# An attention and mixture-of-experts kernel: the copy of transposed q puts tokens in natural order, and each store of the output becomes one block

## The chip, the core and the metric

The kernel runs on one core of a Trainium2 chip. The core has TensorE (PE) for matrix products, VectorE (DVE), ScalarE (ACT) and GpSimd (POOL) for the rest, SyncE (SP), which here only issues transfers, and 16 DMA engines that move data between HBM and the on-chip memory SBUF. TensorE writes its results to PSUM, eight banks of 2 KB in each of 128 partitions. The metric is the device time of one execution in microseconds (us).

## What is computed

```python
q_s = softmax(q, axis=-1)            # q, k, v: (8 batches, 8 heads, 576 tokens, 64)
k_s = softmax(k, axis=2)             # over the tokens
kv  = einsum('bhsd,bhse->bhde', k_s, v)
x   = einsum('bhsd,bhde->bhse', q_s, kv)      # then laid out as (8, 576, 512)

pooled = x.mean(axis=1)              # one row for each batch
logits = pooled @ w_gate             # 8 experts
e      = argmax(logits);  gate = softmax(logits)[e]
out[b] = gate * (relu(x[b] @ w1[e]) @ w2[e])  # w1: 512 x 1024, w2: 1024 x 512
```

The inputs and the output are float32. Each batch picks one expert, and only that expert's weights are loaded.

## The kernel before

**Layout of the tokens.** A load of q, k or v brings four heads of one batch (half a batch, `i`) into a tile of 128 partitions. `pair_src` puts token `9 p + j` of a head into partition `p` (64 of them for each of two heads), at place `j`. So a partition holds nine neighbouring tokens, and the loads read long contiguous rows. TensorE transposes q for each `j` (L150): 64 columns, one for each `p`, go to columns `64 j + p` of a PSUM bank. VectorE copies the 576 columns as they lie to the tile `qt` in SBUF (L157). From there on the columns of x, and so of h, stand in the order `(j, p)`, not in that of the tokens.

**A batch.** `attention(b)` is a generator of ten steps, with a `yield` after each; `moe(b)` has thirteen. Attention: exp of q and k on ScalarE (`eq`, `ek`, L118 and L123); the cast of v on GpSimd (`va`, L129); row sums, reciprocals and the scaling of `eq` on VectorE (`qs`, `qsi`, `eq`, L134 to L137). Then for each half `i`: the transposes (L150, bank `tk`) and the two copies `qt` (L157); k times v (L164), the scaled `kv` (L171, L173); x (L182, L183) and its copy `xt` to SBUF with the sum for the mean (L184, L188). Then the logits (L196), the expert's number (L205), the loads of its weights as float16, issued by GpSimd (`w1_sb`, `w2_sb`, L211 to L217), and the gate (L225 to L231). MoE: eight blocks of 128 hidden units (`hm`, L243, 512 tokens; `ht`, L248, the last 64), each followed by a relu on ScalarE or VectorE in turn (`hsb`, L253 and L255), and then five blocks of output rows (`po`, L264), which ScalarE scales by the gate into `osb` (L269) and SP stores (L271).

**The store.** The five blocks of a batch have 128 columns each, the last 64. A block of 128 columns holds two values of `j`, so its rows are two sets of 64 tokens, each with a step of nine tokens in the output:

```python
out_j = out.rearrange("b (p j) d -> b j p d", j=J)
...
js = slice(2 * st, min(2 * st + 2, J))
nc.sync.dma_start(out=out_j[b, js], in_=osb[0:rows])
```

**The order.** The first two batches' attention runs alone (the opening). Then iteration `b` runs the steps of `moe(b)` in turn with those of `attention(b + 2)`, until in iterations 6 and 7 `moe` is alone. This order is fixed for TensorE; the other engines' order is made by a scheduler. Buffers bound how far things run ahead: three input tiles of each kind (half a batch each), three `eq`, `ek` and `va`, so exp and softmax run up to three half-batches ahead of the transposes; three sets of weights; two banks `hm`, two `tk`, one `x`, two `po`; four `osb`. On SP the loads of batches 0 to 5 stand ahead of the first stores, then come the loads of batch 6, the stores of batch 1, the loads of batch 7, and only stores after that.

Of the kernel before, what the change touches and what calls it, by code (L numbers as in the profile page):

```python
# [10 lines left out]
FP16 = mybir.dt.float16  # L11
# [8 lines left out]
def kernel(  # L20
# [12 lines left out]
    nc = tc.nc  # L33

    B, H, S, Dh = q.shape
    D, E = moe_w_gate.shape
    F = moe_w1.shape[2]
    J = S // 64
# [18 lines left out]
    def bank(tag, bufs):  # L57
        return psum.tile([128, 512], FP32, name=tag, tag=tag, bufs=bufs)
# [33 lines left out]

        return t[b].rearrange("(i n g) (p j) d -> i (g p) n (j d)", i=2, n=2, p=64)[i]


    out_j = out.rearrange("b (p j) d -> b j p d", j=J)

    state = {}
    nv = [0]

# [9 lines left out]
    def attention(b, tiles, roomy):  # L110
# [5 lines left out]
        for i in range(2):  # L116
            eq = e_pool.tile([128, J, 2, Dh], FP16, name="eq")
            nc.scalar.activation(  # L118
                out=eq.rearrange("p j n d -> p n j d"),
                in_=tiles["q", i].rearrange("p n (j d) -> p n j d", j=J), func=AF.Exp,  # L120
# [3 lines left out]
                out=ek.rearrange("p j n d -> p n j d"),  # L124
                in_=tiles["k", i].rearrange("p n (j d) -> p n j d", j=J), func=AF.Exp,
# [4 lines left out]
                out=va[:, :, 1:].rearrange("p j (n d) -> p n j d", n=2),  # L130
                in_=tiles["v", i].rearrange("p n (j d) -> p n j d", j=J),
# [6 lines left out]
                out=eq, in0=eq, in1=qsi.unsqueeze(3).to_broadcast([128, J, 2, Dh]), op=ALU.mult,  # L138
# [5 lines left out]
        for i in range(2):  # L144
            eq, ek, va = eqs[i], eks[i], vas[i]
            tps = [bank(t_tag, 2) for g in range(2)]
            for j in range(J):
                for g in range(2):
                    r = slice(64 * g, 64 * g + 64)
                    nc.tensor.transpose(  # L150
                        out=tps[g].bitcast(FP16)[:, 64 * j:64 * j + 64],
                        in_=eq[r, j], identity=ident[r, r],
                    )
            qts = []
            for g in range(2):
                qt = qt_pool.tile([128, S], FP16, name="qt")
                nc.vector.tensor_copy(out=qt, in_=tps[g].bitcast(FP16)[:, 0:S])  # L157
                qts.append(qt)
            yield
            kps = [bank("tk", 2) for g in range(2)]  # L160
            for j in range(J):
                for g in range(2):
                    r = slice(64 * g, 64 * g + 64)
                    nc.tensor.matmul(  # L164
                        kps[g][:, 0:129], lhsT=ek[r, j], rhs=va[r, j],
                        start=(j == 0), stop=(j == J - 1),
                    )
            kvs = []
            for g in range(2):
                icv = kv_pool.tile([128, 1], FP32, name="icv")  # L170
                nc.vector.reciprocal(out=icv, in_=kps[g][:, 0:1])  # L171
                kv = kv_pool.tile([128, 128], FP16, name="kv")
                nc.vector.scalar_tensor_tensor(  # L173
                    out=kv, in0=kps[g][:, 1:129], scalar=icv, in1=blkmask, op0=ALU.mult, op1=ALU.mult,
                )
                kvs.append(kv)
            yield
            for g in range(2):
                c = 2 * i + g
                px = bank(x_tag, x_bufs)  # L180
                pxt = kps[g][:, 192:256]
                nc.tensor.matmul(px, lhsT=kvs[g], rhs=qts[g][:, 0:SM], start=True, stop=True)  # L182
                nc.tensor.matmul(pxt, lhsT=kvs[g], rhs=qts[g][:, SM:S], start=True, stop=True)  # L183
                nc.vector.tensor_tensor_reduce(  # L184
                    out=xt[:, c, 0:SM], in0=px, in1=ones_f32.to_broadcast([128, SM]),
                    scale=1.0, scalar=0.0, op0=ALU.mult, op1=ALU.add, accum_out=pooled[:, c:c + 1],
                )
                nc.vector.tensor_tensor_reduce(  # L188
                    out=xt[:, c, SM:S], in0=pxt, in1=ones_f32.to_broadcast([128, ST]),
                    scale=1.0, scalar=pooled[:, c:c + 1], op0=ALU.mult, op1=ALU.add,  # L190
                    accum_out=pooled[:, c:c + 1],
                )
                yield
# [15 lines left out]
        for i in range(2):  # L209
            for h in range(2):  # L210
                nc.gpsimd.dma_start(  # L211
                    out=w1_sb[64 * h:64 * h + 64, 2 * i:2 * i + 2, :], in_=w1_src[i, h]
# [22 lines left out]
    def moe(b):  # L235
        xt, gate, w1_sb, w2_sb = state.pop(b)
        hsb = h_pool.tile([128, NF, S], FP16, name="hsb")
        pht = bank("ht", 1)
        for fc in range(NF):
            phm = bank("hm", 2)  # L240
            fsl = slice(fc * 128, (fc + 1) * 128)
            for c in range(ND):
                nc.tensor.matmul(  # L243
                    phm, lhsT=w1_sb[:, c, fsl], rhs=xt[:, c, 0:SM],
                    start=(c == 0), stop=(c == ND - 1),
                )
            for c in range(ND):
                nc.tensor.matmul(  # L248
                    pht[:, fc * ST:(fc + 1) * ST], lhsT=w1_sb[:, c, fsl], rhs=xt[:, c, SM:S],
                    start=(fc == 0 and c == 0), stop=(fc == NF - 1 and c == ND - 1),  # L250
                )
            if fc % 2 == 0:
                nc.scalar.activation(out=hsb[:, fc, 0:SM], in_=phm, func=AF.Relu)  # L253
            else:
                nc.vector.tensor_single_scalar(out=hsb[:, fc, 0:SM], in_=phm, scalar=0.0, op=ALU.max)  # L255
            yield
        nc.scalar.activation(
            out=hsb[:, :, SM:S], in_=pht.rearrange("p (c s) -> p c s", c=NF), func=AF.Relu
        )
        for st in range(5):  # L260
            rows = 128 if st < 4 else ST
            po = bank("po", 2)
            for fc in range(NF):
                nc.tensor.matmul(  # L264
                    po[0:rows], lhsT=hsb[:, fc, st * 128:st * 128 + rows], rhs=w2_sb[:, fc, :],
                    start=(fc == 0), stop=(fc == NF - 1),
                )
            osb = o_pool.tile([128, D], FP32, name="osb")
            nc.scalar.mul(osb[0:rows], po[0:rows], gate[0:rows])  # L269
            js = slice(2 * st, min(2 * st + 2, J))  # L270
            nc.sync.dma_start(out=out_j[b, js], in_=osb[0:rows])  # L271
            yield

    def drain(gen):
# [7 lines left out]
    with tc.manual_schedule(engines={ET.PE}):  # L282
        for b in range(AHEAD):
            drain(attention(b, ins.pop(b), True))
        for b in range(B):
            n = b + AHEAD
            att = iter(())
            if n < B:
                if n not in ins:
                    ins[n] = loads(n)  # L290
                att = attention(n, ins.pop(n), False)
                next(att)
            for step, _ in enumerate(moe(b)):
                next(att, None)
            drain(att)
# [30 lines left out]
```

## Time and profile before

| | |
|---|---|
| time, median of 3 runs | 341.39 us (339.92 to 342.43) |
| the profiled execution, its own time | 341.65 us |
| its span in the profile | 340.0 us |
| mean granted clock of TensorE | 0.85 of full speed |
| moved by the DMA | 54.81 MB, 161 GB/s over the span |
| of it inputs and output (queue q1) | 37.75 MB |
| of it weights, as written (queue q0) | 16.78 MB |

A row of the profile's timeline reads: start in us, duration in us, engine, line, operation, output<-inputs, partitions x elements, count, and in brackets the idle time of the engine just before with what ended it. A row of the groups reads: line, engine, operation, shape, count | busy us, mean ns of one | idle us before. A row of the list of waits reads: engine and line that waited <- what it waited for: us in total, times, the longest. A row of the table of stretches reads: from:to, length, then busy us and count for PE, PEld (TensorE's weight loads), DVE, ACT and POOL, then granted clock, mean busy share of the 16 DMA engines, and GB/s. Overlapping packets can take that share over 1. In the chain, a step is what the last instruction was waiting for, followed back to the start.

### The profile page before, as it was taken

The numbers are of one execution on the slowest core, as the hardware profiler recorded it, in microseconds if no ns is written. First come the engines' busy times: TensorE is split into PE (matmuls) and PEld (weight loads), VectorE is DVE, ScalarE is ACT, GpSimd is POOL, SyncE is SP. The second block draws the span as 40 slices with busy tenths as digits, with TensorE's granted clock in tenths as the row PEclk, the third lists the DMA queues.
The fourth block names the chain that finished last, engine by engine and source line by source line (L and its number), as shares of the span: only waits on it lengthen the run. The fifth ranks groups of instructions, "written<-read, shape, count | busy, mean of one in ns | idle before, by whom it ended". The sixth has DMA issues, their size and how long they took to land.

```text
span 340.0 us, 4144 instructions
## 1 busy us (share of the span) xinstructions
PE 193.5 (57%) x1552; PEld 95.5 (28%) x1552; DVE 123.6 (36%) x365; ACT 89.6 (26%) x130; POOL 52.1 (15%) x73
## 2 busy tenths in 40 slices
PE   0344387880068930889107895960769885479400
PEld 0223144440024420344103443530335341134100
DVE  3699949510058110780106816710236020011000
ACT  2644235210044300442004434210123230123100
POOL 1325261330001410014100141040000400000000
PEclk9999999995559985699755999996779998599955
DMA  7999999999619791199811149179121781112111
GB/s 262 396 391 378 278 294 280 290 284 285 139 65 332 197 187 36 58 338 223 149 36 64 41 80 196 43 140 166 37 67 52 140 150 38 65 51 66 51 64 42
DMA packets 31508, 54.81 MB, mean 161 GB/s; under 512 B 2304, under 2 KB 10496, under 8 KB 31488
## 3 DMA queue, kind: packets, MB, share of 16 engines
q1 hardware_dynamic: 17856, 37.75, 31.4%
q0 software_dynamic: 13056, 16.78, 29.3%
q8 instruction: 12, 0.20, 0.2%
q10 hardware_dynamic: 576, 0.02, 0.1%
q14 instruction: 8, 0.07, 0.1%
HBM read 61.88 MB, written 9.44 MB: 210 GB/s over the span
## 4 chain that ended last, share of the span: by engine, by line
DMA 48%; DVE 19%; PE 18%; ACT 5%; issue 2%; SPq 1%; ACTq 1%; POOL 0%; DVEq 0%; POOLq 0%
DMA out_dram<-osb 45%; PE hm L243 8%; DVE qs L134 5%; PE po L264 5%; DVE eq L137 4%; DVE xt L184 3%; ACT osb L269 2%; DMA wg_sb<-in_moe_w_gate_dram 2%; DVE hsb L255 2%; ACT eq L118 2%; PE x L182 1%; DMA v_in<-in_v_dram 1%; DVE kv L173 1%; SPq L271 1%; ACT hsb L253 1%
## 5 line engine op out<-in xcount | busy, mean ns | idle before, releaser
L243 PE MATMUL hm<-xt,w_sb 128*128 128x512 f16 x256 | 74.5, 421 | 60.9 <-ACT hsb L253 60.9
L264 PE MATMUL po<-w_sb,hsb 128*128 128x512 f16 (+1 forms) x320 | 77.8, 393 | 22.9 <-ACT osb L269 22.9
L269 ACT ACTIVATE osb<-po,gate 128x512 f32<-128x512 f32 (+1 forms) x40 | 27.2, 686 | 151.6 <-DMA out_dram<-osb 120.8
L264 PEld LDWEIGHTS <-hsb 128*128 128x128 f16 (+1 forms) x320 | 31.0, 103 | 61.0 <-issue 31.3
L243 PEld LDWEIGHTS <-w_sb 128*128 128x128 f16 x256 | 22.5, 105 | 88.0 <-issue 72.6
L134 DVE TENSOR_REDUCE qs<-eq 128x18 f32<-128x1152 f16 x16 | 21.5, 1345 | 64.9 <-ACT eq L118 64.9
L129 POOL CAST va<-v_in 128x1152 f16<-128x1152 f32 x16 | 19.7, 1239 | 132.7 <-PE tk L164 82.2
L255 DVE TENSOR_SCALAR hsb<-hm 128x512 f16<-128x512 f32 x32 | 22.1, 690 | 44.6 <-PE hm L243 44.0
L211 POOL DMA_DIRECT2D w_sb<-in_moe_w_dram x32 | 19.3, 623 | 81.6 <-DVE gt L225 39.6
L253 ACT ACTIVATE hsb<-hm 128x512 f16<-128x512 f32 x32 | 18.8, 588 | 41.8 <-PE hm L243 41.8
L157 DVE COPY qt<-tk 128x576 f16<-128x576 f16 x24 | 9.9, 453 | 52.7 <-PE tk L150 52.7
L248 PEld LDWEIGHTS <-w_sb 128*128 128x128 f16 x256 | 17.7, 104 | 18.1 <-issue 5.4
L137 DVE TENSOR_TENSOR eq<-eq,qsi 128x1152 f16<-128x1152 f16 x16 | 21.8, 1360 | 0.1
L118 ACT ACTIVATE eq<-q_in 128x1152 f16<-128x1152 f32 x16 | 18.6, 1160 | 9.8 <-DMA q_in<-in_q_dram 5.7
L123 ACT ACTIVATE ek<-k_in 128x1152 f16<-128x1152 f32 x16 | 18.5, 1157 | 7.5 <-PE tk L164 4.2
L248 PE MATMUL ht<-xt,w_sb 128*128 128x64 f16 x256 | 19.2, 200 | 0.0
L184 DVE CUSTOM_DVE_ANT_0 xt<-x,ones_f 128x512 f16<-128x512 f32 x24 | 16.4, 684 | 6.6 <-PE tk L183 6.6
L182 PE MATMUL x<-qt,kv 128*128 128x512 f16 x24 | 10.8, 449 | 11.6 <-DVE kv L173 7.0
L164 PE MATMUL tk<-va,ek 64*128 64x129 f16 x288 | 13.8, 246 | 2.9 <-DVE pooled L188 1.9
L164 PEld LDWEIGHTS <-ek 64*128 64x128 f16 x288 | 10.5, 108 | 4.1 <-issue 2.1
L150 PEld LDWEIGHTS <-eq 64*128 64x128 f16 x288 | 6.4, 103 | 12.6 <-issue 11.8
L182 PE MATMUL po<-qt,kv 128*128 128x512 f16 x8 | 4.4, 612 | 9.3 <-DVE kv L173 9.3
(49 smaller groups left out, 106.1 us busy)
## 6 DMA issues: line engine op xcount, KB each, us to landing
q_in<-in_q_dram SPq DMA_DIRECT2D x16, 576.0 KB
k_in<-in_k_dram SPq DMA_DIRECT2D x16, 576.0 KB
v_in<-in_v_dram SPq DMA_DIRECT2D x16, 576.0 KB
w_sb<-in_moe_w_dram POOLq DMA_DIRECT2D x32, 256.0 KB, 10.6
w_sb<-in_moe_w_dram POOLq DMA_DIRECT2D x16, 512.0 KB, 20.7
out_dram<-osb SPq DMA_DIRECT2D x32, 256.0 KB
out_dram<-osb SPq DMA_DIRECT2D x8, 128.0 KB
wg_sb<-in_moe_w_gate_dram ACTq DMA_DIRECT2D x4, 4.0 KB
```

Source lines behind the costliest of these rows:

```text
L118: nc.scalar.activation(out=eq.rearrange("p j n d -> p n j d"), in_=tiles["q", i].rearrange("p n (j d) -> p n j d", j=J), func=AF.Exp,)
L129: nc.gpsimd.tensor_copy(out=va[:, :, 1:].rearrange("p j (n d) -> p n j d", n=2), in_=tiles["v", i].rearrange("p n (j d) -> p n j d", j=J),)
L134: nc.vector.tensor_reduce(out=qs, in_=eq, op=ALU.add, axis=AX.X)
L137: nc.vector.tensor_tensor(out=eq, in0=eq, in1=qsi.unsqueeze(3).to_broadcast([128, J, 2, Dh]), op=ALU.mult,)
L164: nc.tensor.matmul(kps[g][:, 0:129], lhsT=ek[r, j], rhs=va[r, j], start=(j == 0), stop=(j == J - 1),)
L184: nc.vector.tensor_tensor_reduce(out=xt[:, c, 0:SM], in0=px, in1=ones_f32.to_broadcast([128, SM]), scale=1.0, scalar=0.0, op0=ALU.mult, op ...
L243: nc.tensor.matmul(phm, lhsT=w1_sb[:, c, fsl], rhs=xt[:, c, 0:SM], start=(c == 0), stop=(c == ND - 1),)
L248: nc.tensor.matmul(pht[:, fc * ST:(fc + 1) * ST], lhsT=w1_sb[:, c, fsl], rhs=xt[:, c, SM:S], start=(fc == 0 and c == 0), stop=(fc == NF - ...
L253: nc.scalar.activation(out=hsb[:, fc, 0:SM], in_=phm, func=AF.Relu)
L255: nc.vector.tensor_single_scalar(out=hsb[:, fc, 0:SM], in_=phm, scalar=0.0, op=ALU.max)
L264: nc.tensor.matmul(po[0:rows], lhsT=hsb[:, fc, st * 128:st * 128 + rows], rhs=w2_sb[:, fc, :], start=(fc == 0), stop=(fc == NF - 1),)
L269: nc.scalar.mul(osb[0:rows], po[0:rows], gate[0:rows])
```

## The change

The copy out of PSUM now reads column `64 j + p` and writes column `9 p + j`, so `qt`, x and h have the tokens in natural order. The source is read in steps of 64 elements, the destination written in sequence. A block of output rows is then 128 (or 64) neighbouring tokens, and the store writes them as one contiguous block.

```diff
-    out_j = out.rearrange("b (p j) d -> b j p d", j=J)
...
-                nc.vector.tensor_copy(out=qt, in_=tps[g].bitcast(FP16)[:, 0:S])
+                nc.vector.tensor_copy(
+                    out=qt.rearrange("q (p j) -> q p j", j=J),
+                    in_=tps[g].bitcast(FP16)[:, 0:S].rearrange("q (j p) -> q p j", j=J),
+                )
...
-            js = slice(2 * st, min(2 * st + 2, J))
-            nc.sync.dma_start(out=out_j[b, js], in_=osb[0:rows])
+            nc.sync.dma_start(out=out[b, st * 128:st * 128 + rows, :], in_=osb[0:rows])
```

The number of instructions stays the same on each engine. The order of TensorE, ScalarE, GpSimd and SP stays too; lines of the changed kernel are numbered up to three lower. On SP, around the first stores (`out_dram<-osb`, with the shape of the destination), there stands before:

```order
L106 DMA k_in<-in_k_dram 128x2x576
L106 DMA v_in<-in_v_dram 128x2x576
L271 DMA out_dram<-osb 2x64x512 x4
L271 DMA out_dram<-osb 64x512
L106 DMA q_in<-in_q_dram 128x2x576
```

and now:

```order
L103 DMA k_in<-in_k_dram 128x2x576
L103 DMA v_in<-in_v_dram 128x2x576
L270 DMA out_dram<-osb 128x512 x4
L270 DMA out_dram<-osb 64x512
L103 DMA q_in<-in_q_dram 128x2x576
```

Nothing has moved; the four 128-row stores of each batch have another shape, and the 64-row store has the same one.

On VectorE the scheduler orders the opening differently. After the second half of batch 0 is transposed, there stands before:

```order
L157 COPY qt<-hm 128x576 x2
L134 TENSOR_REDUCE qs<-eq 128x18
L171 RECIPROCAL icv<-tk 128x1 x2
L136 RECIPROCAL qsi<-qs 128x18
L173 SCALAR_TENSOR_TENSOR kv<-tk,icv,blkmask 128x128 x2
L137 TENSOR_TENSOR eq<-eq,qsi 128x1152
L184 ISA xt,pooled<-po,ones_f_100 128x512
```

and now:

```order
L154 COPY qt<-hm 128x576 x2
L171 RECIPROCAL icv<-tk 128x1 x2
L131 TENSOR_REDUCE qs<-eq 128x18
L173 SCALAR_TENSOR_TENSOR kv<-tk,icv,blkmask 128x128 x2
L133 RECIPROCAL qsi<-qs 128x18
L184 ISA xt,pooled<-po,ones_f_100 128x512
```

The scaling of a later `eq` has moved behind the copies `xt` there. There are a few more such exchanges up to the gate of batch 1; as many `qs` and `eq` stand ahead of that gate as before (seven of each), and from there on the order is the same.

## The prediction

> **What bounds the kernel now.** I read the page first: busy shares, DMA queues, chain.
>
> ```profile
> PE 193.5 (57%) x1552; PEld 95.5 (28%) x1552; DVE 123.6 (36%) x365; ACT 89.6 (26%) x130; POOL 52.1 (15%) x73
> q1 hardware_dynamic: 17856, 37.75, 31.4%
> q0 software_dynamic: 13056, 16.78, 29.3%
> DMA out_dram<-osb 45%; PE hm L243 8%; DVE qs L134 5%; PE po L264 5%; DVE eq L137 4%; DVE xt L184 3%; ACT osb L269 2%; DMA wg_sb<-in_moe_w_gate_dram 2%; DVE hsb L255 2%; ACT eq L118 2%; PE x L182 1%; DMA v_in<-in_v_dram 1%; DVE kv L173 1%; SPq L271 1%; ACT hsb L253 1%
> ```
>
> No engine is busy for more than 57% of the span, and the 16 DMA engines together for 60.7% (31.4 + 29.3). Yet 45% of the chain that ended last is the output stores. The list of waits, by total, says who suffers:
>
> ```profile
> ACT osb L269 <- DMA out_dram<-osb: 120.8, 14, 23.8
> ...
> PE hm L243 <- ACT hsb L253: 60.9, 7, 20.7
> ```
>
> ScalarE waits 120.8 us for an osb buffer that a store still reads. Behind that osb in ScalarE's queue stands the next batch's first relu (hsb), and TensorE, out of its two hm banks, waits 60.9 us for it. Why stores are slow shows in the table of stretches (the columns after the five engines are granted clock, DMA share, GB/s):
>
> ```profile
> 20.00:30.00 10.00, 3.01 (x38) 1.85 (x40) 9.54 (x28) 4.23 (x6) 2.31 (x3) 1.00 1.05 390
> 110.00:120.00 10.00, 10.00 (x61) 4.46 (x61) 1.49 (x11) 3.14 (x6) 3.90 (x6) 1.00 0.84 208
> 290.00:300.00 10.00, 6.18 (x20) 2.29 (x20) 0.00 (x0) 1.95 (x3) 0.00 (x0) 0.69 0.13 51
> 324.00:330.00 6.00, 0.00 (x0) 0.00 (x0) 0.00 (x0) 0.00 (x0) 0.00 (x0) 0.50 0.13 51
> ```
>
> At 20 to 30 us only loads run: 1.05 of 16 engines, 390 GB/s, so 23 GB/s an engine. At 324 to 330 only stores run: 0.13 x 16 = 2.1 engines and 51 GB/s, 24.5 GB/s an engine. The engines are not slow; a store keeps two of them busy. A 128-row store (262,144 B) takes 262,144 / 51 GB/s = 5.14 us. Late in the kernel the period of five stores is the distance of two 64-row osb's, both held by a store:
>
> ```profile
> 302.10 0.68 ACT L269 ACTIVATE osb<-po,gate 64x512 f32<-64x512 f32 x1 [4.18 <-DMA out_dram<-osb]
> ...
> 323.26 0.68 ACT L269 ACTIVATE osb<-po,gate 64x512 f32<-64x512 f32 x1 [4.18 <-DMA out_dram<-osb]
> ```
>
> It is 21.16 us, of which four 128-row stores take 20.56. The fifth, of 64 rows, gets 0.6 us; on two engines it would need 2.57. It is the one store that already is one block of rows, so the row order decides, not the direction of the transfer.
>
> The page "DMA: Bandwidth & Descriptors" of the Trainium skill, section "Why a DMA increments its semaphore by 16 and not by 1", says that a transfer runs on the largest number of engines up to 16 that divides the slowest dimension of both access patterns: 2 for a destination of 2 x 64 x 512, 16 for 128 x 512. The 2.1 busy engines agree; that 128-row stores spread no run here shows yet.
>
> **The change, part by part.**
>
> **The stores.** The destination goes from 2 x 64 x 512 to 128 x 512; 32 of 40 stores change. At 390 GB/s one takes 0.7 us, and even shared with loads some 2 us, against a new osb every 1.80 us with four buffers. I take it that ScalarE's 120.8 us of waits go, and TensorE's with them. What is late next is the work itself, so I rebuild the span from stretches without store waits. Unhindered is iteration 0 (MoE of batch 0 beside attention of batch 2):
>
> ```profile
> 44.60 1.89 PE L243 MATMUL hm<-xt,w_sb 128*128 128x512 f16 x4
> ...
> 49.26 1.16 PE L164 MATMUL tk<-va,ek 64*128 64x129 f16 x18
> ...
> 56.09 1.04 PE L243 MATMUL hm<-xt,w_sb 128*128 128x512 f16 x4
> ...
> 66.25 5.47 PE L264 MATMUL po<-w_sb,hsb 128*128 128x512 f16 x24
> 71.66 1.04 PE L243 MATMUL hm<-xt,w_sb 128*128 128x512 f16 x4
> ...
> 74.20 0.70 PE L164 MATMUL tk<-va,ek 64*128 64x129 f16 x18
> ```
>
> It runs from 44.60 to 71.66: 27.06 us. Its start is slow: from the first hm to the first tk (L164) takes 49.26 - 44.60 = 4.66 against 74.20 - 71.66 = 2.54 an iteration later, and that tk group 1.16 against 0.70. Warm, the iteration is 27.06 - 2.12 - 0.46 = 24.5. Later iterations of the trace start slow too, since TensorE idles in the store waits (granted clock 0.50 at 324 to 330 us); in a stretch with TensorE busy throughout (110 to 120) it is 1.00, so I count them warm.
>
> Softmax of q runs three half-batches ahead, so the second half of iteration 4 and all of iteration 5 have none. In iteration 5 the second half is
>
> ```profile
> 254.87 1.04 PE L243 MATMUL hm<-xt,w_sb 128*128 128x512 f16 x4
> ...
> 268.69 1.04 PE L243 MATMUL hm<-xt,w_sb 128*128 128x512 f16 x4
> ```
>
> 13.82 us long, against 71.66 - 56.09 = 15.57 in iteration 0: 1.75 less for each such half. Iterations 6 and 7 are MoE alone:
>
> ```profile
> 306.25 1.03 PE L243 MATMUL hm<-xt,w_sb 128*128 128x512 f16 x4
> ...
> 308.21 1.03 PE L243 MATMUL hm<-xt,w_sb 128*128 128x512 f16 x4
> ```
>
> Two hm blocks take 1.96, so eight take 7.8; three po blocks take 71.66 - 66.25 = 5.41, so five take 9.0: 16.8 us.
>
> **The copy of q (L157).** It now reads PSUM in steps of 64 elements. No row shows such a read.
>
> ```profile
> L184 DVE CUSTOM_DVE_ANT_0 xt<-x,ones_f 128x512 f16<-128x512 f32 x24 | 16.4, 684 | 6.6 <-PE tk L183 6.6
> L157 DVE COPY qt<-tk 128x576 f16<-128x576 f16 x24 | 9.9, 453 | 52.7 <-PE tk L150 52.7
> L188 DVE CUSTOM_DVE_ANT_0 xt<-tk,ones_f,pooled 128x64 f16<-128x64 f32 x32 | 8.8, 281 | 2.2
> L137 DVE TENSOR_TENSOR eq<-eq,qsi 128x1152 f16<-128x1152 f16 x16 | 21.8, 1360 | 0.1
> ```
>
> Low end: 453 ns as now. High end: 1360, the longest VectorE row. Between them, PSUM reads that get no fast rate: 684 ns for 512 elements and 281 for 64 are 0.90 ns an element and 223 fixed, so 741 for 576. I take 741, the nearest rows: +0.29 us a copy, 32 copies.
>
> Here a rule of the Trainium skill speaks against the change: "VectorE: DVE Perf Modes", section "What auto-detection actually checks", grants the paired rate only where every 16-bit tensor has step 1, which this read loses. By its cycle table (section on the TRN2 errata) the copy goes from an estimated 425 ns (the row says 453) to 725; the sum would be under 1 us lower than with 741.
>
> In the first 44 us VectorE is busy 9.54 of 10, so eight copies cost 8 x 0.29 = 2.3 us there. The scheduler also reorders softmax steps there, but as many of them stand ahead of batch 1's gate; I count that as nothing, with 2 us either way. In an iteration, where a copy matters shows in the second half of iteration 0:
>
> ```profile
> 56.18 0.82 DVE L157 COPY qt<-tk 128x576 f16<-128x576 f16 x2 [0.50 <-PE tk L150]
> 57.16 0.69 DVE L255 TENSOR_SCALAR hsb<-hm 128x512 f16<-128x512 f32 x1 [0.16 <-PE hm L243]
> ...
> 59.33 0.51 DVE L173 SCALAR_TENSOR_TENSOR kv<-tk,icv,blkmask 128x128 f16<-128x128 f32 x2
> ```
> ```profile
> 59.64 0.39 PE L182 MATMUL x<-qt,kv 128*128 128x512 f16 x1 [0.68 <-DVE kv L173]
> ```
>
> Two copies grow by 0.58; 0.16 of it hides in the wait of hsb for TensorE; the remaining 0.42 moves hsb, qs and kv, and TensorE, already 0.68 us idle for kv, waits that much longer. So 0.42 for each half with softmax. In the three halves without, VectorE has a qs (1.35 us) less to do, which covers it: nothing.
>
> **The first stores.** SP issues in program order:
>
> ```profile
> 67.43 2.94 SPq L106 DMA_DIRECT2D v_in<-in_v_dram  x1
> 70.46 29.38 SPq L271 DMA_DIRECT2D out_dram<-osb  x5
> ```
> ```profile
> 63.94 0.69 ACT L269 ACTIVATE osb<-po,gate 128x512 f32<-128x512 f32 x1 [2.27 <-PE po L264]
> ```
> ```profile
> 75.00:80.00 5.00, 0.00 (x0) 0.00 (x0) 0.00 (x0) 0.00 (x0) 1.16 (x1) 0.78 1.09 273
> ```
>
> The first osb is ready at 64.6, but its store goes out at 70.5, behind the loads of batch 5, and the DMA is full (1.09) until 80. The new store waits behind those three loads: 3 x 590 KB at 273 GB/s is 6.5 us, so it lands near 78, and the fifth osb, wanted at about 75, is some 3 us late. TensorE covers part with two hm blocks (2.5 us). I take 2 us once, between 0 and 6.
>
> **The end.** After the last po: osb 0.69, then a store that has the engines to itself. No row shows one. At 2.1 engines' rate it would take 2.6 us, and a whole round of loads took
>
> ```profile
> 106.39 4.73 DMA v_in<-in_v_dram
> ```
>
> 4.73 from issue to landing. I take 3 us, together 3.7.
>
> **Sum.** 44.6 + 2.3 = 46.9 to the first MoE matmul; iteration 0: 27.06 + 0.84 = 27.9; 1 to 3: 3 x (24.5 + 0.84) = 76.0; 4: 24.5 - 1.75 + 0.42 = 23.2; 5: 24.5 - 3.5 = 21.0; 6 and 7: 33.6; first stores 2; end 3.7. That is 234.3 us of span. The profiled execution took 341.65 for a span of 340.0, so 1.65 on top: **236 us**. It stands 0.3 above the median of 341.39, so nothing is corrected.
>
> **Rivals.**
>
> *The strided read is dearer than one element a step.* At 1360 ns the copy adds 0.91: 5.0 more in the opening, (1.82 - 0.16 - 0.42) = 1.24 more in each of nine halves, about 0.5 in the three others: 236 + 5.0 + 11.2 + 1.5 = 254. For it: nothing here reads PSUM in steps. Against: the rows that read PSUM one element at a time, at 0.90 ns each.
>
> *The DMA becomes the bound.* 60.7% of 340 us is 206 us of all 16 engines; at the full share of 1.09 that is 189 us, 45 less than my span, so not as a whole. But a batch needs 206 / 8 / 1.09 = 23.7 us of DMA in an iteration of 25.3 while inputs still load (iterations 0 and 1). If weights or fifth osb's then wait 4 to 5 us in each: 245.
>
> *VectorE hides the copies and the stalls of 0.68 vanish with the better overlap.* With copies at 453 ns the sum loses 2.3 + 9 x 0.42: 230; without the first-store wait and a slightly shorter end, 227.
>
> *The store still uses two engines*, or its rate hangs on something else than the engine count. Then the period of 21.16 us stays and only the opening grows: 341.65 + 2.3 = 344. Against it stands the 64-row store's 0.6 us.
>
> *Slower: a single block is put on one engine.* Each 128-row store then takes 262,144 / 24.5 GB/s = 10.7 us; 32 of them and 8 short ones from 70.5 on end at 70.5 + 342 + 5 = 418, 419 in all. It decides as soon as a store gets less than the 51 GB/s of now. Against: the 64-row block is not so treated.
>
> **Chances.** Forecast 0.62 (230 to 243); dear copy 0.12; DMA bound 0.11; hidden copies 0.10; still two engines 0.03; one engine 0.02. The range 227 to 254 takes in the first four cases, nearly, and the bounds of the copy. Faster by over 1% 0.95, within 1% (about what a measurement of this kernel can tell from no change) 0.02, slower 0.03.
>
> **What would show it.** Stores: ScalarE's wait of 120.8 us for out_dram under 10, a store stretch above 0.13 of DMA share, stores under 10% of the chain. Copies: L157's successor at 0.7 to 0.8 us. Iterations: 25 us from first hm to first hm in 1 to 3, 17 in 6 and 7; granted clock 1.00 after 45 us. First stores: one wait of ScalarE near 75 us. Wrong it is if the copy shows over 1 us, if TensorE waits for weights, or if the stores still hold ScalarE.

## The result and the profile after

| | before | after |
|---|---|---|
| time, median | 340.77 us | 253.59 us (252.31 to 253.92) |
| ratio to before | | 0.743, interval 0.739 to 0.747 |
| span of the profiled execution | 340.0 us | 251.7 us |
| mean granted clock of TensorE | 0.85 | 0.96 |

The change gains 87 us; the forecast was 236, the range 227 to 254. The page of the changed kernel, busy shares and chain:

```profile
PE 184.3 (73%) x1552; PEld 92.9 (37%) x1552; DVE 131.4 (52%) x365; ACT 91.1 (36%) x130; POOL 52.5 (21%) x73
...
PE po L264 27%; PE hm L243 12%; DMA out_dram<-osb 8%; DVE qt L154 8%; DVE qs L131 8%; DVE eq L134 7%; DVE xt L184 5%; DVE hsb L255 3%; DMA wg_sb<-in_moe_w_gate_dram 2%; DVE kv L173 2%; PE tk L147 2%; PE x L182 1%; DVE xt L188 1%; PE ht L248 1%; DVE qsi L133 1%
```

Matrix products lead the chain; the stores fell from 45% to 8%. What is left of them is one event. The list of waits:

```profile
ACT osb L269 <- DMA out_dram<-osb: 19.6, 1, 19.6
...
PE hm L243 <- ACT hsb L253: 16.0, 1, 16.0
...
PE tk L164 <- DVE qt L154: 2.9, 11, 0.3
```

ScalarE's wait for stores went from 120.8 us in 14 pieces to 19.6 in one. On ScalarE's timeline it is the fifth osb of batch 0:

```profile
71.18 0.69 ACT L269 ACTIVATE osb<-po,gate 128x512 f32<-128x512 f32 x1 [1.04 <-PE po L264]
91.44 0.68 ACT L269 ACTIVATE osb<-po,gate 64x512 f32<-64x512 f32 x1 [19.57 <-DMA out_dram<-osb]
```

and in the chain, the first store of the kernel, with the stretches that it spans:

```profile
70.52 20.81 DMA out_dram<-osb
```
```profile
70.00:75.00 5.00, 5.00 (x43) 2.28 (x41) 0.53 (x1) 0.82 (x2) 1.24 (x2) 1.00 1.11 284
75.00:80.00 5.00, 1.37 (x24) 0.95 (x23) 1.49 (x3) 0.00 (x0) 1.17 (x1) 0.85 1.09 275
80.00:85.00 5.00, 0.00 (x0) 0.00 (x0) 0.00 (x0) 0.00 (x0) 0.00 (x0) 0.50 1.13 292
85.00:90.00 5.00, 0.00 (x0) 0.00 (x0) 0.00 (x0) 0.00 (x0) 0.00 (x0) 0.50 1.13 288
```

The DMA engines are full all the while (1.09 to 1.13) with other transfers, and TensorE does nothing from 80 to 90 us; its clock falls to 0.50. The strided copy in the groups (line, shape, count | busy us, mean ns):

```profile
L154 DVE COPY qt<-tk 128x576 f16<-128x576 f16 x24 | 17.1, 753 | 38.9 <-PE tk L147 38.9
```

753 ns, against 453 before and 741 forecast. The iterations start, on TensorE's timeline, with the first hm (L243) at 45.63, 72.92, 116.23, 141.85, 167.46, 191.44, 213.98 and 230.67 us. Two of these rows:

```profile
116.23 0.39 PE L243 MATMUL hm<-xt,w_sb 128*128 128x512 f16 x1
```
```profile
141.85 0.39 PE L243 MATMUL hm<-xt,w_sb 128*128 128x512 f16 x1
```

Iteration 2 takes 25.6 us.

### The profile page after: what moved, and what is told of

It reads as the page before. It is cut to its first block, busy times and chain, and to the rows that moved or that the text cites. A ratio compares the mean times of both kernels' runs of the same rounds, so it can differ in the third digit from the quotient of the medians.

```text
span 251.7 us, 4145 instructions
## 1 busy us (share of the span) xinstructions
PE 184.3 (73%) x1552; PEld 92.9 (37%) x1552; DVE 131.4 (52%) x365; ACT 91.1 (36%) x130; POOL 52.5 (21%) x73
## 4 chain that ended last, share of the span: by engine, by line
PE 47%; DVE 37%; DMA 11%; ACT 2%; issue 1%; ACTq 1%; DVEq 0%
PE po L264 27%; PE hm L243 12%; DMA out_dram<-osb 8%; DVE qt L154 8%; DVE qs L131 8%; DVE eq L134 7%; DVE xt L184 5%; DVE hsb L255 3%; DMA wg_sb<-in_moe_w_gate_dram 2%; DVE kv L173 2%; PE tk L147 2%; PE x L182 1%; DVE xt L188 1%; PE ht L248 1%; DVE qsi L133 1%
## 5 line engine op out<-in xcount | busy, mean ns | idle before, releaser
L243 PE MATMUL hm<-xt,w_sb 128*128 128x512 f16 x256 | 69.0, 397 | 16.0 <-ACT hsb L253 16.0
L264 PE MATMUL po<-w_sb,hsb 128*128 128x512 f16 (+1 forms) x320 | 73.4, 380 | 0.0
L264 PEld LDWEIGHTS <-hsb 128*128 128x128 f16 (+1 forms) x320 | 29.9, 100 | 35.0 <-issue 3.4
L154 DVE COPY qt<-tk 128x576 f16<-128x576 f16 x24 | 17.1, 753 | 38.9 <-PE tk L147 38.9
L243 PEld LDWEIGHTS <-w_sb 128*128 128x128 f16 x256 | 20.9, 100 | 39.9 <-issue 21.9
L248 PEld LDWEIGHTS <-w_sb 128*128 128x128 f16 x256 | 16.8, 101 | 16.4 <-issue 2.2
L164 PE MATMUL tk<-va,ek 64*128 64x129 f16 x288 | 16.0, 246 | 5.0 <-DVE qt L154 2.9
L248 PE MATMUL ht<-xt,w_sb 128*128 128x64 f16 x256 | 18.5, 196 | 0.0
L182 PE MATMUL x<-qt,kv 128*128 128x512 f16 x24 | 9.6, 401 | 10.8 <-DVE pooled L184 5.8
L164 PEld LDWEIGHTS <-ek 64*128 64x128 f16 x288 | 11.3, 108 | 7.7 <-issue 6.5
```

The lines of the kernel that those rows point to most:

```text
L154: nc.vector.tensor_copy(out=qt.rearrange("q (p j) -> q p j", j=J), in_=tps[g].bitcast(FP16)[:, 0:S].rearrange("q (j p) -> q p j", j=J),)
L164: nc.tensor.matmul(kps[g][:, 0:129], lhsT=ek[r, j], rhs=va[r, j], start=(j == 0), stop=(j == J - 1),)
L243: nc.tensor.matmul(phm, lhsT=w1_sb[:, c, fsl], rhs=xt[:, c, 0:SM], start=(c == 0), stop=(c == ND - 1),)
L248: nc.tensor.matmul(pht[:, fc * ST:(fc + 1) * ST], lhsT=w1_sb[:, c, fsl], rhs=xt[:, c, SM:S], start=(fc == 0 and c == 0), stop=(fc == NF - ...
L264: nc.tensor.matmul(po[0:rows], lhsT=hsb[:, fc, st * 128:st * 128 + rows], rhs=w2_sb[:, fc, :], start=(fc == 0), stop=(fc == NF - 1),)
```

## The experiments

**Only the copy.** The kernel before, with the new copy alone:

```diff
-                nc.vector.tensor_copy(out=qt, in_=tps[g].bitcast(FP16)[:, 0:S])
+                nc.vector.tensor_copy(
+                    out=qt.rearrange("q (p j) -> q p j", j=J),
+                    in_=tps[g].bitcast(FP16)[:, 0:S].rearrange("q (j p) -> q p j", j=J),
+                )
```

> The kernel before with only the copy changed: PSUM is read in steps, tokens go in natural order, but the store keeps its old destination of 2 x 64 x 512 (so the output rows land at other tokens' places). Theory 'the number of DMA engines a store uses': nothing is gained, the copy costs a little in the opening only, 341 to 344 us, a batch of stores still takes 21.2 us late in the kernel. Rival 'the natural order of tokens itself helps' : below 330 us.

343.57 us against 342.96 for before on the same chip: ratio 1.0027 (1.0010 to 1.0043). The order of the tokens by itself gains nothing. The five stores of a batch still take 324.53 - 303.40 = 21.1 us, between two 64-row osb's on ScalarE's timeline:

```profile
303.40 0.68 ACT L272 ACTIVATE osb<-po,gate 64x512 f32<-64x512 f32 x1 [4.19 <-DMA out_dram<-osb]
...
324.53 0.68 ACT L272 ACTIVATE osb<-po,gate 64x512 f32<-64x512 f32 x1 [4.20 <-DMA out_dram<-osb]
```

**One block, but two engines.** The changed kernel; the same 128 neighbouring output rows, written in another form:

```diff
-            nc.sync.dma_start(out=out[b, st * 128:st * 128 + rows, :], in_=osb[0:rows])
+            dst = out[b, st * 128:st * 128 + rows, :]
+            if st < 4:
+                dst = dst.rearrange("(p a) d -> a p d", a=2)
+            nc.sync.dma_start(out=dst, in_=osb[0:rows])
```

> The changed kernel, but each 128-row store goes to the same 128 neighbouring output rows in the form 2 x 64 x 512: even rows from partitions 0 to 63, odd ones from 64 to 127 (rows within a block of 128 are permuted). The block as a whole is still one piece of memory. Theory 'the slowest dimension sets the engines': two engines, 51 GB/s, 341 to 345 us. Rival 'rows nine tokens apart were the trouble': 252 to 256 us.

343.51 us, against 341.98: ratio 1.0034 (1.0010 to 1.0058). All of the gain is gone, with the rows of a store still neighbours in memory. On ScalarE's timeline the period is back, 325.33 - 304.07 = 21.3 us:

```profile
304.07 0.68 ACT L269 ACTIVATE osb<-po,gate 64x512 f32<-64x512 f32 x1 [4.18 <-DMA out_dram<-osb]
...
325.33 0.68 ACT L269 ACTIVATE osb<-po,gate 64x512 f32<-64x512 f32 x1 [4.20 <-DMA out_dram<-osb]
```

**Eight.** The same edit with `a=8`.

> As the run with 2 x 64 x 512, in the form 8 x 16 x 512 (rows within a block are permuted). Theory 'the slowest dimension sets the engines': eight engines, about 8 x 24.5 = 196 GB/s and 1.3 us for a store alone, still less than the 1.8 us between two osb's: 253 to 257 us. Rival 'any form but one block is slow': above 300 us.

255.06 us (two runs, 254.42 and 255.71), ratio 0.746 (0.742 to 0.750). Eight engines are enough, then, also with rows that are out of sequence in the block. That the store runs on eight engines shows on the page, in the number of small packets (under 512 B). First before (2304, as in the run with 2 x 64 x 512 on one block), then here, then in the changed kernel:

```profile
DMA packets 31508, 54.81 MB, mean 161 GB/s; under 512 B 2304, under 2 KB 10496, under 8 KB 31488
```
```profile
DMA packets 31700, 54.81 MB, mean 216 GB/s; under 512 B 2496, under 2 KB 10688, under 8 KB 31680
```
```profile
DMA packets 31956, 54.81 MB, mean 218 GB/s; under 512 B 2752, under 2 KB 10944, under 8 KB 31936
```

The 32 large stores have 192 and 448 small packets more than before, 6 and 14 each. One small packet for each engine that a store uses, with two engines before, makes that 8 and 16.

**Rows apart, but 16 engines.** The kernel before, with its copy and its order of tokens; each 128-row store issued as two:

```diff
-            js = slice(2 * st, min(2 * st + 2, J))
-            nc.sync.dma_start(out=out_j[b, js], in_=osb[0:rows])
+            for j in range(2 * st, min(2 * st + 2, J)):
+                r = slice(64 * (j - 2 * st), 64 * (j - 2 * st) + 64)
+                nc.sync.dma_start(out=out_j[b, j], in_=osb[r])
```

> The kernel before (old copy, old token order, rows nine tokens apart), but each 128-row store is issued as two of 64 rows, one for each j, each with 64 as its slowest dimension. Theory 'a store uses as many engines as its slowest dimension allows': as fast as the changed kernel without its dearer copy, 247 to 250 us. Rival 'the output block must be contiguous': 330 us or more.

249.51 us, ratio 0.728 (0.726 to 0.731). The small packets are 3264, 30 more than before for each block: two stores on 16 engines instead of one on two. So a contiguous block is neither needed nor enough: rows that lie nine tokens apart go as fast once the slowest dimension of the transfer is 64 instead of 2.

**The copy's price.** The changed kernel with the copy of before (the output rows come in another order):

```diff
-                nc.vector.tensor_copy(
-                    out=qt.rearrange("q (p j) -> q p j", j=J),
-                    in_=tps[g].bitcast(FP16)[:, 0:S].rearrange("q (j p) -> q p j", j=J),
-                )
+                nc.vector.tensor_copy(out=qt, in_=tps[g].bitcast(FP16)[:, 0:S])
```

> The changed kernel with the copy of before (no steps; the output rows are then in another token order). It prices the strided copy. Theory 'the longer copy delays kv, 0.42 us in each of nine half-batches, plus 1 us in the opening': 253.6 - 5 = 248.6 us. Rival 'VectorE's slack hides the copy': 253 us. In both the first store still holds ScalarE for some 19 us.

249.40 us, ratio 0.727 (0.725 to 0.730): 4.2 us less than the changed kernel, across two chips. Its profiled execution took 251.56 us, 2.2 over the median, and the wait for the first store is 2.6 us longer in it than in the changed kernel:

```profile
ACT osb L266 <- DMA out_dram<-osb: 22.2, 1, 22.2
```

Part of what the copy gives back is lost to this wait, as the run with two stores of 64 rows shows, which has the old copy too and was profiled at its median: its iteration 2 starts at 115.28 us, 0.95 earlier than in the changed kernel, while with ten buffers (below) the old copy brings it forward by 2.38, from 99.08 to 96.70.

**The first store: more buffers.** The changed kernel with `tc.tile_pool(name="o", bufs=10)` in place of 4.

> The changed kernel with 10 osb buffers in place of 4. The first store is issued at 70.5 us and lands 20.8 us later; ScalarE waits 19.6 us for its buffer. Theory 'the first stores queue behind loads, and only the buffer makes it matter': with ten buffers nobody waits, and TensorE's slow restart goes too, 253.6 - 17 to 19 = 235 us, as the prediction's sum with 2 us for that place. Rival 'the DMA is the bound there, and the wait moves to weights, inputs or the stores after': 247 us or more.

236.06 us (235.84 to 236.32), ratio 0.689 (0.687 to 0.691). No osb waits for a store any more (that row is gone from the list of waits; one of 0.5 us, for an eq, names a store), TensorE's clock is 1.00 over the whole span, and the first MoE iteration is followed by one of 25.6 us, from 73.47 to 99.08:

```profile
73.47 1.04 PE L243 MATMUL hm<-xt,w_sb 128*128 128x512 f16 x4
```
```profile
99.08 1.04 PE L243 MATMUL hm<-xt,w_sb 128*128 128x512 f16 x4
```

The store itself is not faster. The longest landing of a store (the view of the output tensor, from issue, min/median/max) is 20.8 us in the changed kernel and 20.9 with ten buffers:

```profile
DMA to landing us min/median/max: 2.0/4.3/20.8
```
```profile
DMA to landing us min/median/max: 2.0/7.4/20.9
```

**The first store: another queue.** The changed kernel with `nc.scalar.dma_start` for the store, so that ScalarE issues it; loads stay on SP.

> The changed kernel with the stores issued by ScalarE, right behind each osb, instead of SP; loads stay on SP, four osb buffers. Theory 'the first store waits in the rings of SP's queue behind loads issued earlier': on a queue of its own it lands within some 6 us, the fifth osb does not wait, 236 to 240 us (each issue costs ScalarE some 0.3 to 0.7 us, beside waits for po). Rival 'the DMA engines are full until 90 us whichever queue a store is in': it lands some 20 us after issue, and the time stays above 246 us.

245.09 us, ratio 0.717 (0.714 to 0.720): 8.5 less than the changed kernel, but 5 more than the top of what was expected. The part that it was to decide is decided. With the DMA as full as ever (1.08 to 1.14 from 65 to 95 us), no store takes longer than 8.3 us:

```profile
DMA to landing us min/median/max: 2.0/5.1/8.3
```

So the 20.8 us come from SP's queue, and full engines alone do not explain them: the first store stood behind loads that had been issued before it. What ate the rest of the gain sits in iteration 1, which takes 32.3 us instead of the 25.6 with ten buffers, and there is a new wait in it:

```profile
55.68 25.60 DMA v_in<-in_v_dram
81.35 0.54 ACTq L270
```
```profile
81.94 0.60 ACT L253 ACTIVATE hsb<-hm 128x512 f16<-128x512 f32 x1 [4.08 <-DMA v_in<-in_v_dram]
```

The fifth store's issue on ScalarE (ACTq L270, from the chain) starts only when a load of v has landed that SP issued 25.6 us earlier. The trace names the semaphore (a counter that engines wait on) that each transfer raises when it lands: the transfers of SP and ScalarE use eight of them in turn. The third, fourth and fifth stores have those of the loads of q, k and v issued at 50.57, 53.27 and 55.68 us, and each goes out within 0.1 us of that load's landing. No run took this wait away alone.

**One buffer more.** `bufs=5` in the changed kernel.

> The changed kernel with 5 osb buffers in place of 4. Theory 'only the fifth osb of batch 0 waits for the first store': one more buffer is enough, and the next user of the first buffer comes an iteration later, when the store has just landed: 236 to 238 us, as with ten. Rival 'several buffers are held at once in that stretch': 241 us or more.

236.08 us (235.78 to 236.11), ratio 0.690 (0.687 to 0.693): all of the 17.5 us for one buffer of 256 KB. One wait of 3.4 us remains.

**Both together.** The two stores of 64 rows, the old copy, and ten buffers; then five.

> The kernel before with each 128-row store issued as two of 64 rows, and 10 osb buffers; the old copy. Against the changed kernel with 10 buffers (236.06 us) it prices the strided copy without the first-store wait. By the prediction's terms, 0.42 us in nine half-batches and 1 us in the opening: 236.1 - 4.8 = 231.3 us. Rival 'the copy is hidden': 235 us or more.

> The kernel before with two stores of 64 rows for each block of 128 and 5 osb buffers (old copy). By both findings, stores on 16 engines without the strided copy, and one buffer more: 231 to 233 us. Rival 'with the shorter opening and iteration the first buffer is wanted earlier than the store lands': 235 us or more.

231.00 us, ratio 0.675 (0.673 to 0.678), and 232.16, ratio 0.678 (0.675 to 0.681), where the wait left is

```profile
ACT osb L269 <- DMA out_dram<-osb: 5.5, 2, 5.2
```

5.2 us in one piece. The version with ten beats both kernels, and the changed one by 22.6 us. Against the changed kernel with ten buffers it prices the strided copy without the first store in the way: 5.1 us, across two chips, and with the other form of the stores in it. The 4.8 expected took the opening's 1 us from the changed kernel's trace; with the prediction's own 2.3 there it would be 6.1.

## Why the prediction was right, and where it was not

**The bound and the stores: right.** Two engines instead of 16 were the greater part of the 45%; 23.8 us of those 153, the first store's piece, had in the main another cause (below). Contiguity is not the cause: the runs with 2 x 64 x 512 on one block (343.51) and with 64-row stores on scattered rows (249.51) separate the two. The Trainium skill, "DMA: Bandwidth & Descriptors", section "Why a DMA increments its semaphore by 16 and not by 1", gives 2, 8 and 16 engines for these forms, and the times and the numbers of small packets agree. The prediction's own inference from the fast 64-row store, "so the row order decides", was wrong: that store's rows lie nine tokens apart like all others of the kernel before, and what sets it apart is the 64 as its slowest dimension.

**The rival of one engine, and that of no effect: fallen.** The 128-row store lands in a median of 4.1 us, with other transfers beside it; one engine alone would have needed 10.7, by the prediction's figure.

**The iterations: right within 8%, all but iteration 1.** 25.6 where 25.3 was forecast (2 and 3), 24.0 for 23.2, 22.5 for 21.0, 16.7 for 16.8. Iteration 0 took 27.3 for 27.9.

**The copy: right in size, partly in the wrong place.** 753 ns, where the prediction took 741 from the nearest rows. The Trainium skill, "VectorE: DVE Perf Modes", section "What auto-detection actually checks", gives the paired rate to 16-bit tensors with a step of 1 or -1. By the page's cycle table the copy was to go from an estimated 425 ns to 725; the trace has 453 and 753. In the half-batches without softmax the prediction had it hidden. There it is on the chain:

```profile
199.34 0.46 PE tk L147 x17
199.79 1.42 DVE qt L154 x2
201.22 0.04 issue
201.26 0.69 PE tk L164 x17
201.94 0.97 PE hm L243 x4
```

The products k times v (L164) go to the bank `tk` that the copy reads, so they wait for the copy; the prediction followed the copy only through VectorE's own queue. With ten buffers the list of waits has 2.9 us in 11 pieces of `tk` for `qt`, and with ten buffers and the old copy no such row. New copy against old, both with ten buffers, it costs 22.54 - 21.59 = 0.95 us in iteration 5 where nothing was forecast, 0.82 instead of 0.42 in iteration 4, 0.70 instead of 0.84 in each of 1 to 3, and 0.06 instead of 0.84 in iteration 0. That the sum of the iterations comes out, 3.9 us for 3.8, is luck: the misses cancel. The opening was priced too high: first hm at 45.63, 1.0 later than before, where 2.3 was forecast (45.63 to 46.57 over all runs with the new copy, 44.45 to 45.20 with the old one).

**The first stores: the step that failed.** "The new store waits behind those three loads: 3 x 590 KB at 273 GB/s is 6.5 us", and of that 2 us in the time, between 0 and 6. The store landed 20.8 us after its issue, and iteration 1 took 43.3 us instead of 25.6: 17.7 for 2. The semaphores tell what was under way: when it was issued, at 70.52 us, six loads had not landed, not three, those issued at 50.43, 54.17, 57.84, 58.36, 64.55 and 67.32. They landed in this order, at 73.7, 77.6, 81.1, 84.0, 86.9 and 89.9, and the store behind them at 91.3. Six loads are 3.5 MB of the 5 x (284 + 275 + 292 + 288) = 5.7 MB that the DMA moved from 70 to 90 us; the rest, over a third of it, is in the main weights, for which the 6.5 us, taken at the full rate, leave no room. The prediction counted the loads whose issue it saw last, not those that had not landed; in the trace of before the same six landed from 73.6 to 90.0. A row that would have told stood there too: the first store's piece in the chain, 23.80 us from 70.46, is 4.6 times the 5.14 us that its two engines need. With 17.7 in place of the 2 us, 236 becomes 252. Two of the prediction's own signs told of it: ScalarE's wait for stores was to be under 10 us and was 19.6, and the granted clock was to be 1.00 after 45 us and fell to 0.50 from 80 to 90. With the buffers that take the wait away, the run gave 236.06: the rest of the sum came out, its misses of up to 1.5 us in a term cancelling.

**The range** held the time by 0.4 us, and that is luck: its upper part was made for a dearer copy and for a DMA that is the bound, and neither happened. The rival of a full DMA named the fifth osb's among those who wait, but priced it from the DMA's total load, at 4 to 5 us in each of two iterations; it was one wait, from a backlog in one queue.

## What to carry to other kernels

Read the DMA busy share of a stretch in which only one kind of transfer runs, and turn it into a number of engines: here 2 of 16 meant that the outermost dimension of the access pattern was too short, and a change of its form, or two issues instead of one, was all that it took. When a wait of many pieces is to be taken away, look at each of its long pieces by itself: they can have different causes, and the one with another cause stays. A transfer that is issued behind loads made far ahead pays for their backlog, so what it holds needs one buffer more, or the transfer another queue.

## What the runs showed of the hardware

Transfers issued by SP landed in the order of their issue where the DMA was full: a store behind six loads landed after 20.8 us, and on ScalarE's queue no store took over 8.3. A 128-row store used as many engines as its form allowed: 2 for 2 x 64 x 512 (51 GB/s), 8 for 8 x 16 x 512, 16 for 128 x 512, with as many small packets. A read of PSUM in steps of 64 float16 elements costs 753 ns for 576, about what reads element by element give (0.90 ns an element and 223 fixed, from the rows of before, make 741). The fastest store landed 2.0 us after its issue.
